# A Strassen feed-forward layer behind retention: the order in which the weights of the first layer are converted

## The chip, the cores and the metric

The kernel runs on one core of a Trainium2 chip. The metric is the device time of one execution in microseconds (us), from the first to the last work of the core. A core has five engines with a queue each, and every queue is worked off in the order in which the program issued it: TensorE (PE in the profile; its weight loads are shown apart as PEld), VectorE (DVE), ScalarE (ACT), GpSimd (POOL) and SyncE (SP), which here issues nearly all transfers. Engines wait for each other through semaphores.

## What is computed

Two layers, one behind the other (8 batches, 8 heads, 576 positions, head size 64; 4608 tokens, model width 512, inner width 2048):

```
scores = q k^T / sqrt(64);  ret = scores * gamma_h^(i-j) for i >= j, else 0;  attn = ret v
x = attn as [4608, 512]
h = max(x w_in, 0);  out = (h * h) w_out          # w_in 512 x 2048, w_out 2048 x 512
```

The two weights arrive as 64-bit floating point numbers. [...]the kernel converts them itself, with integer and 32-bit operations on the two halves of each number.

## The kernel before

**Stages.** Retention works through 40 chunks (per batch four of 128 positions and one of 64). Four chunks make a block of 512 tokens; there are nine blocks. The first layer of the feed-forward part runs beside retention. For block 0 it is a plain product (`first_in`, 16 of them, one per converted piece of 512 x 128 weights). Blocks 1 to 8 use Strassen's seven products (`ffn_in`, L758), whose inputs are sums of weight pieces and so need all of the weights. The second layer (`inner`, L1094) follows when retention is over.

**The order is written out by hand.** The program is under a manual schedule: each engine does its work in program order. The list of feed-forward products is `steps`; `step()` issues the next one. `convert(n)` issues the next n parts of the weight conversion. A prologue of single lines (L898 to L953) does chunks 0 to 3 and the first four pieces; then a loop over the chunks calls `ffn(i, half)` at the two halves of each chunk, which for block 0 issues one or two `first_in` and six conversion parts with each.

**One piece of the conversion** (`round_parts`, L213 to L231) has these parts:

- `one` (L213, VectorE): takes the exponent out of the high word.
- `two` (L217, VectorE): takes the upper fraction bits out of the high word.
- `beside` (L221 and L222, ScalarE, two instructions): makes a float of the low word, and a scale of the exponent. L222 needs `one` of the same piece; L221 needs only the loaded raw data.
- `three` (L225, VectorE): adds the two fractions; needs `two` and L221.
- `four` (L228, VectorE): multiplies by the scale; needs L222.
- `five` (L231, VectorE), issued by `last`: puts the sign on. After it the piece is ready for `first_in`, and `last` also asks for the next raw piece by a transfer.

In the kernel before, pieces 0 to 2 go one, two, beside, three, four, last. From piece 3 on `one` and `two` of the next piece are put between `beside` and `three` of this one (`N_ALONE`).

**What stands around it in the queues.** `first_in(j)` (L722) issues eight TensorE instructions of 128x512 (pieces 0 and 1 in halves and quarters), then the eviction of the result on ScalarE (`Relu`, L727), and puts the squaring (L730, VectorE) into a list from which the next product takes two. `turn` transposes a chunk's q and k on TensorE (L439) and copies them out of PSUM in two halves, with `(0, 1)` one on ScalarE and one on VectorE, with `(0, 0)` both on ScalarE (L450; L453 for chunks of 64). `scores_full` and `scores` (L547, L480) need both copies. `masked` (L492) or the mask in `scores_full` (L551) is VectorE's; `retain_full` (L573, L576) and the retain functions of the loop need it. `x_out` copies the chunk's result on ScalarE (L594), and `grown` the state (L506). `scale_q` (L385) and `scale_v` (L499) multiply loaded chunks by decays on GpSimd. `warm(n)` (L885) issues n products of 256 columns, of two TensorE instructions each, whose results nobody reads.

In the loop the parts of one call of `convert(6)` are three, four, last of a piece, beside of the next, and one, two of the one after that. In the first half of a chunk the six parts come ahead of the product, in the second half behind it.

Of the kernel before, what the change touches and what calls it, by code (L numbers as in the profile page):

```python
# [40 lines left out]
def kernel(  # L41
# [89 lines left out]
    N_EARLY = TOK // C  # L131

    def load(i, names="qkv"):
        b, ci, c0, cs = chunks[i]
        if i == 0:
            nc.sync.dma_start(dv, decays)
        got = loaded.setdefault(i, [None] * 3)
        for name, pool, src in (("q", ld3, q), ("k", ld5, k), ("v", ld4, v)):
            if name not in names:
                continue  # L140
            t = got["qkv".index(name)] = pool.tile([128, H, D], F32, tag=name, name=f"{name}_ld")

            issue = nc.scalar if i == 0 and name != "q" else nc.sync
            at = src[b, :, c0:c0 + cs, :].rearrange("h s d -> s h d")
            if name == "v":
                issue.dma_start(t[:cs], at)
            else:

                for e in range(2):
                    issue.dma_start(t[:cs, e * HP:(e + 1) * HP, :], at[:, e::2, :])  # L150
# [5 lines left out]
    pieces = [(0, m, e) for m in range(N_M) for e in range(2)]  # L156
    pieces += [(1, mq + mh * N_MQ, e) for mq in range(N_MQ) for mh in range(2) for e in range(2)]
    N_W1 = N_DF
    N_ALONE = 3
    N_HALF = 2  # L160
    stage = [W[5].rearrange("p (o s f) -> p o s f", o=4, s=NP),
             W[6][:, 0:3 * NP * 128].rearrange("p (o s f) -> p o s f", o=3, s=NP)]
# [5 lines left out]
    def raw_of(j):  # L168
        return raw_all[j % N_RAW] if j < N_W1 else raw_all[(j - N_W1) % 3]

    def exp_of(j):
        return exp_all[j % 2] if j < N_W1 else exp_all[2 * (j % 2)]
# [18 lines left out]
    def as_dst(j, t):  # L191

        if pieces[j][0] == 0:
            return t.rearrange("p (c f) -> p c f", c=N_DM)
        return t.rearrange("p (o s f) -> p o s f", o=2, s=2)
# [8 lines left out]
    def round_parts(j):  # L204
        words = raw_of(j).bitcast(U32).rearrange("p (n two) -> p n two", two=2)
        lo, hi = words[:, :, 0], words[:, :, 1]
        frac = raw_of(j).rearrange("p (n two) -> p n two", two=2)[:, :, 0]
        exp = exp_of(j).bitcast(U32)
        t = piece_dst(j)
        bits = t.bitcast(U32)  # L210

        def one():
            nc.vector.tensor_scalar(exp, hi, 20, 0x7FF, op0=ALU.logical_shift_right, op1=ALU.bitwise_and)  # L213

        def two():

            nc.vector.tensor_scalar(bits, as_dst(j, hi), 0xFFFFF, 0x100000, op0=ALU.bitwise_and, op1=ALU.bitwise_or)  # L217

        def beside():

            nc.scalar.activation(frac, lo, AF.Copy, scale=2.0 ** -52)  # L221
            nc.scalar.activation(exp, exp, AF.Relu, bias=exp_bias[:, 0:1], scale=2.0 ** 23)  # L222

        def three():
            nc.vector.scalar_tensor_tensor(t, bits, 2.0 ** -20, as_dst(j, frac), op0=ALU.mult, op1=ALU.add)  # L225

        def four():
            nc.vector.tensor_tensor(t, t, as_dst(j, exp_of(j)), op=ALU.mult)  # L228

        def five():  # L230
            nc.vector.scalar_tensor_tensor(bits, as_dst(j, hi), 0x80000000, bits, op0=ALU.bitwise_and, op1=ALU.bitwise_or)  # L231

        if not wide:
            to = t if pieces[j][0] == 0 else t.rearrange("p o s f -> p (o s) f")
            return [lambda: nc.sync.dma_start(to, piece_src(j))] + [lambda: None] * 5
        return [one, two, beside, three, four, five]
# [60 lines left out]

    def w_in_parts():

        parts = [round_parts(j) for j in range(N_W1)] + [[None] * 2]  # L300
        for j in range(N_W1):
            one, two, beside, three, four, five = parts[j]
            if j <= N_ALONE:
                yield from (one, two)
            yield beside
            if j >= N_ALONE:
                yield from parts[j + 1][0:2]
            yield three
            yield four

            def last(five=five):
                five()
                n_made[0] += 1
                if n_next[0]:
                    fetch_raw(2)

            yield last
# [3 lines left out]
    def convert(count):  # L321
        for _ in range(count):
            f = next(w_in_steps, None)
            f and f()
# [130 lines left out]
    def turn(i, engines=(0, 1)):  # L455
        turn_in(i)
        turn_out(i, engines)
# [99 lines left out]
    def carry_full(i):  # L557

        xp[0] = ps_x.tile([128, 2, 256], F32, tag="x", name="x_ps", padded_shape=[128, 2, 512])
        clean.clear()  # L560
        if chunks[i][1] == 0:
            u_ps[0] = ps_u.tile([128, HP, D], F32, tag="u", name="u_ps")
            return
        u = u_sb[2 * chunks[i][1] % 3]
        for hp, e, b in HEADS[0:2] + HEADS[4:6] + HEADS[2:4] + HEADS[6:8]:
            nc.tensor.matmul(x_full(hp, e, b), lhsT=u[rows(e), hp, :], rhs=st[i]["qT"][rows(e), hp, :],
                             start=clears(b, e), stop=False, skip_group_check=True)

    def retain_full(i):

        ci = chunks[i][1]
        for hp, e, b in (HEADS[j] for j in (0, 4, 2, 6, 1, 5, 3, 7)):
            nc.tensor.matmul(x_full(hp, e, b), lhsT=st[i]["vs"][:, head(hp, e), :], rhs=st[i]["ret"][:, e, hp, :],  # L573
                             start=clears(b, e), stop=False, skip_group_check=True)
        for hp, e, b in HEADS:
            nc.tensor.matmul(u_ps[0][rows(e), hp, :], lhsT=loaded[i][1][:, 2 * hp + e, :], rhs=st[i]["vs"][:, head(hp, e), :],  # L576
                             start=(ci == 0 and hp == 0), stop=(hp == HP - 1), skip_group_check=True)
        x_out(i, lambda: grown(i, 1))
# [232 lines left out]
    steps = []  # L811
# [12 lines left out]
    def step():  # L824
        n, f, *args = steps.pop(0)
        done[0] += 1
        f(*args)
# [14 lines left out]
    def ffn(i, half):  # L842

        gone[0] += chunks[max(0, min(i, N_CH - 1))][3] / 2
        if half == 2:
            gone[0] += chunks[min(i + 1, N_CH - 1)][3] / 2
        if steps and steps[0][0] == 0:

            move(6)
            for f in (step, lambda: convert(6)) if half else (lambda: convert(6), step):  # L850
                f()
            if half and i > N_EARLY and steps and steps[0][0] == 0:
                step()
                convert(6)
            return
        if not behind:
            behind.append((gone[0] - HALF, done[0]))
        points = behind + [p for p in PACE if p[0] > behind[0][0]]
        want = points[-1][1]
        for (x0, y0), (x1, y1) in zip(points, points[1:]):  # L860
            if gone[0] < x1:
                want = y0 + (y1 - y0) * (gone[0] - x0) / (x1 - x0)
                break
        count = max(1, int(want) - done[0])
        while steps and count:
            held[0] = half != 1 and count <= (1 if half else 2)

            if half == 2:
                due = sum(m[0] <= i + 2 for m in moves)
                move(max(2, min(4, -(-due // (count - 1)))) if count > 1 else 0)  # L870
            else:
                move(4 if half and len(moves) > 8 else 3 if half else 2 if count > 1 else 0)
            busy[0] = len(flips) > 0
            for f in flips[:1]:
                f()
            del flips[:1]
            step()
            count -= 1
        held[0] = busy[0] = False


    def warm(count):
        t = ps_f.tile([128, 512], F32, tag="f", name="idle_ps")
        for _ in range(count):
            nc.tensor.matmul(t[:, 0:256], lhsT=idle, rhs=idle[:, 0:1].to_broadcast([128, 256]), start=True, stop=True)  # L885
# [13 lines left out]
    scale_q(0, nc.vector)  # L899
    turn_in(0, (1,))  # L900
    scale_q(1, nc.gpsimd)
    warm(3)
    turn_in(0, (0,))
    turn_out(0)
    load(3)
# [2 lines left out]
    scores_full(0)  # L908
    turn(1, (0, 0))
    carry_full(0)  # L910
    retain_full(0)
    convert(3)
    scores_full(1)
    scale_q(2, nc.gpsimd)
    carry_full(1)
    convert(3)
    retain_full(1)
    load(4)
    fetch_raw(3)
# [6 lines left out]
    scale_q(3, nc.gpsimd)  # L926
    carry_full(2)
    first_in(1, (0,))
    convert(3)
    retain_full(2)  # L930
    load(6)
    turn(3)
    scores_full(3)
    scale_q(4, nc.gpsimd)
    convert(3)
    carry_full(3)
    for j in range(N_HALF):
        first_in(j, (1,), (0, C))
    early.close()
    ps_t[0] = first.enter_context(tc.tile_pool(name="ps_t", bufs=1, space=PS))  # L940
    retain_full(3)
    load(7)
    convert(5)
    step()
    step()
    turn(4)
    convert(3)
    step()
    scores(4)
    scale_q(5, nc.gpsimd)  # L950
    convert(6)
    step()
    convert(3)  # L953
    for i in range(N_EARLY + 1, N_CH + 1):
# [219 lines left out]
    for k in range(N_K + 1):  # L1174
# [5 lines left out]
        for e in range(3):  # L1180
# [8 lines left out]
            if sums_g:  # L1189
                f = sums_g.pop(0)  # L1190
            else:
                f = next(steps_0, None)
# [52 lines left out]
```

## Time and profile before

| what | value |
|---|---|
| median of three runs | 964.96 us (964.32 to 965.64) |
| span of the profiled execution | 963.2 us |
| PE, PEld busy | 98%, 88% |
| DVE, ACT, POOL busy | 81%, 35%, 14% |
| first product of block 0 to start (L722) | 18.0 us |
| last product of block 0 to start (piece 15) | 100.5 us |
| first product of block 1 to start (L758) | 105.7 us |

The table's last three rows come from the order of time: the conversion of the first weights and everything that the change touches lie in the first 106 us of 963 us. The rest of the span is block 1 to 8 of the first layer and the second layer, which the change leaves as they are. Where TensorE stands idle in those 106 us can be read from two views: the list of waits, limited to that stretch, and the order of time of one engine, which gives behind each group the idle time ahead of it and what ended it.

### The profile page before, as it was taken

To read this page: it belongs to the slowest core of one execution; us is meant where nothing else is said; L and a number is where in the kernel's file an instruction comes from. 1 tells how busy PE (TensorE), PEld (TensorE's weight loads), DVE (VectorE), ACT (ScalarE), POOL (GpSimd) and SP (SyncE) were. 2 spreads that over 40 slices of the span, in tenths; PEclk is the share of its full clock that TensorE was granted. 3 is DMA by queue.
4 is the path that set the end of the run, shared out by engine and by line. 5 is a ranking of instruction groups with operands and counts; after the bars stand their busy time and mean duration, and the time that the engine had idled before them with its cause. 6 is when DMAs were issued, how large, how long until landed. Compare 5 with 4: busy or idle time off the path is not lost. (4 is left out here: it accounts for less than half of the span.)

```text
span 963.2 us, 23158 instructions
## 1 busy us (share of the span) xinstructions
PE 947.4 (98%) x9754; PEld 849.4 (88%) x9754; DVE 784.6 (81%) x1446; ACT 337.4 (35%) x807; POOL 134.5 (14%) x123
## 2 busy tenths in 40 slices
PE   8999999999999999999999999999999999999998
PEld 6644688888888888888888899999999999999998
DVE  5788799888799887987966588888888787787876
ACT  3444375866765766667621010000000000000000
POOL 3311323214123123122110000000000000000000
PEclk9999999999999999999999999999999999999999
DMA  9983567676757867774278966445454454525251
GB/s 224 259 246 102 147 180 197 190 236 199 206 149 222 243 147 208 211 224 148 81 261 331 357 246 246 149 149 186 137 181 166 173 189 162 197 100 176 88 176 44
DMA packets 170728, 181.37 MB, mean 188 GB/s; under 512 B 116864, under 2 KB 131200, under 8 KB 163968
## 3 DMA queue, kind: packets, MB, share of 16 engines
q1 hardware_dynamic: 168528, 179.37, 59.5%
q8 instruction: 76, 1.25, 0.5%
q10 hardware_dynamic: 2096, 0.52, 0.3%
q14 instruction: 28, 0.23, 0.1%
HBM read 109.36 MB, written 70.52 MB: 187 GB/s over the span
## 5 line engine op out<-in xcount | busy, mean ns | idle before, releaser
L758 PE MATMUL h_b<-room,w 128*128 128x256 f32 x768 | 183.7, 382 | 2.3 <-DVE room L777 1.8
L422 ACT COPY qk<-flip 32x256 f32<-32x256 f32 x416 | 167.4, 402 | 6.1
L758 PEld LDWEIGHTS h_b<-room,w 128*128 128x128 f32 x768 | 144.1, 190 | 24.0 <-DVE room L777 3.3
L1094 PE MATMUL o_b<-w,room 128*128 128x128 f32 x1168 | 144.4, 275 | 0.2 <-DVE room L1046 0.2
L1094 PEld LDWEIGHTS o_b<-w,room 128*128 128x128 f32 x1168 | 137.3, 192 | 0.4 <-DVE room L1046 0.4
L1094 PE MATMUL o_c<-w,room 128*128 128x128 f32 x1008 | 123.0, 275 | 0.0
L758 PE MATMUL h_a<-room,w 128*128 128x256 f32 x512 | 122.1, 381 | 0.0
L758 PE MATMUL h_c<-room,w 128*128 128x256 f32 x512 | 121.7, 380 | 0.0
L1094 PEld LDWEIGHTS o_c<-w,room 128*128 128x128 f32 x1008 | 117.7, 192 | 0.0
L1108 ACT COPY r<-o_a 128x128 f32<-128x128 f32 x53 | 14.1, 266 | 271.6 <-PE o_a L1094 236.0
L758 PEld LDWEIGHTS h_a<-room,w 128*128 128x128 f32 x512 | 96.4, 190 | 13.8 <-issue 0.4
L758 PEld LDWEIGHTS h_c<-room,w 128*128 128x128 f32 x512 | 96.7, 190 | 13.3
L1094 PE MATMUL o_a<-w,a 128*128 128x128 f32 x688 | 85.6, 275 | 0.0
L775 POOL TENSOR_TENSOR room<-room 128x512 f32<-128x512 f32 x32 | 35.9, 1123 | 334.5 <-ACT room L774 334.5
L1094 PEld LDWEIGHTS o_a<-w,a 128*128 128x128 f32 x688 | 81.2, 192 | 0.1
L765 DVE SCALAR_TENSOR_TENSOR room<-room 128x512 f32<-128x512 f32 x96 | 70.6, 736 | 3.3
L722 PE MATMUL h_ps<-room,w 128*128 128x512 f32 (+2 forms) x160 | 59.9, 519 | 5.8 <-DVE w L231 5.6
L385 POOL TENSOR_TENSOR q_ld<-q_ld,dv 128x512 f32<-128x512 f32 (+1 forms) x39 | 46.4, 1189 | 85.7 <-DMA q_ld<-in_q_dram 85.5
L499 POOL TENSOR_TENSOR v_ld<-v_ld,dv 128x512 f32<-128x512 f32 (+1 forms) x40 | 52.9, 1323 | 6.7 <-DMA v_ld<-in_v_dram 6.7
L722 PEld LDWEIGHTS h_ps<-room,w 128*128 128x128 f32 x160 | 26.7, 190 | 30.2 <-issue 20.4
L617 PEld LDWEIGHTS x_ps<-qk,v_ld 64*64 64x64 f32 x1024 | 38.8, 134 | 13.0 <-issue 12.3
L777 DVE TENSOR_TENSOR room<-h_b,room 128x512 f32<-128x512 f32 x32 | 21.9, 685 | 33.5 <-PE h_b L758 33.5
(115 smaller groups left out, 1378.0 us busy)
## 6 DMA issues: line engine op xcount, KB each, us to landing
g_dram<-room SPq DMA_DIRECT2D x32, 1280.0 KB, 5.7
a<-g_dram SPq DMA_DIRECT2D x30, 1024.0 KB, 5.9
room<-g_dram SPq DMA_DIRECT2D x15, 1024.0 KB, 6.0
w<-w_dram SPq DMA_DIRECT2D x7, 1792.0 KB, 10.9
out_dram<-room SPq DMA_DIRECT2D x17, 512.0 KB, 3.2
q_ld<-in_q_dram SPq DMA_DIRECT2D x64, 128.0 KB, 5.3
w<-in_moe_w_in_dram SPq DMA_DIRECT2D x16, 512.0 KB, 6.4
w<-in_moe_w_out_dram SPq DMA_DIRECT2D x16, 512.0 KB, 4.1
```

The source lines that it names most:

```text
L385: engine.tensor_tensor(t, t, dv[:cs, :, NCH + ci:NCH + ci + 1].to_broadcast([cs, H, D]), op=ALU.mult)
L422: nc.scalar.copy(*moves.pop(0)[2:])
L499: nc.gpsimd.tensor_tensor(vs[:cs], vs[:cs], dv[:cs, :, ci:ci + 1].to_broadcast([cs, H, D]), op=ALU.mult)
L617: return [lambda hp=hp, e=e, b=b: nc.tensor.matmul(x_at(hp, e, b, h), lhsT=s["vs"][rows(h), head(hp, e), :], rhs=s["ret"][rows(h), e, hp, ...
L722: nc.tensor.matmul(p, lhsT=w[:, c, :], rhs=xT[0][:, c, :].rearrange("p (h t) -> p h t", h=2)[:, lo:hi, at[0]:at[1]], start=(c == 0), stop= ...
L758: nc.tensor.matmul(p[:, mm, :], lhsT=w[:, c, :], rhs=xs[n][right][:, c, :], start=(j in OPENS and mm == 0 and c == 0), stop=(j in CLOSES a ...
L765: nc.vector.scalar_tensor_tensor(t, t, 0.0, t, op0=ALU.max, op1=ALU.mult)
L775: nc.gpsimd.tensor_tensor(g["A11"], g["A11"], g["A11"], op=ALU.mult)
L777: nc.vector.tensor_tensor(g["A22"], p, p15, op=ALU.add)
L1094: nc.tensor.matmul(p, lhsT=s["lefts"][left][:, m, :], rhs=w_out[j][:, m, WO_SLOT[right], :], start=(i in OPENS and m == 0), stop=(i in CLO ...
L1108: nc.scalar.copy(r[:, 0, 0:128], p)
```

## The change

The order of the conversion's parts is changed, and nothing of what they compute.

- `w_in_parts` yields one, two, beside, three, four, last for every piece; `N_ALONE` goes.
- The prologue's calls of `convert` are cut and placed anew. Piece 0's first three parts stand ahead of the eviction of chunk 0 (in `retain_full(0)`) instead of behind it, its `three` follows there, and `four` and `last` come ahead of `retain_full(1)`. Piece 2 is converted ahead of `turn(3)` (before: its last three parts behind `scores_full(3)`), piece 3 ahead of `turn(4)` (before: its last three parts behind it), piece 4 and the first half of piece 5 ahead of the loop.
- In the loop a call of `convert(6)` is now three, four, last of a piece, then one, two, beside of the next: ScalarE's two instructions are issued at the call's end, a call ahead of the `three` that needs them. Every call stands ahead of its product, and so ahead of that product's eviction on ScalarE, in both halves of a chunk.
- The second `warm` call issues one product instead of three.

Its purpose is that weights are ready earlier, that ScalarE's parts don't wait behind evictions, and that fewer products are made for nothing.

```diff
-            one, two, beside, three, four, five = parts[j]
-            if j <= N_ALONE:
-                yield from (one, two)
-            yield beside
-            if j >= N_ALONE:
-                yield from parts[j + 1][0:2]
-            yield three
-            yield four
+            one, two, beside, three, four, five = round_parts(j)
+            yield from (one, two, beside, three, four)
...
             move(6)
-            for f in (step, lambda: convert(6)) if half else (lambda: convert(6), step):
-                f()
-            if half and i > N_EARLY and steps and steps[0][0] == 0:
-                step()
-                convert(6)
+            for _ in range(2 if half and i > N_EARLY else 1):
+                if steps and steps[0][0] == 0:
+                    convert(6)
+                    step()
...
-    warm(3)
+    warm(1)
...
     carry_full(0)
+    convert(3)
     retain_full(0)
-    convert(3)
+    convert(1)
     scores_full(1)
     scale_q(2, nc.gpsimd)
     carry_full(1)
-    convert(3)
+    convert(2)
     retain_full(1)
...
     first_in(1, (0,))
-    convert(3)
+    convert(2)
     retain_full(2)
     load(6)
+    convert(4)
     turn(3)
     scores_full(3)
     scale_q(4, nc.gpsimd)
-    convert(3)
     carry_full(3)
...
+    convert(2)
     retain_full(3)
     load(7)
-    convert(5)
+    convert(1)
     step()
     step()
+    convert(3)
     turn(4)
+    step()
     convert(3)
-    step()
     scores(4)
     scale_q(5, nc.gpsimd)
-    convert(6)
+    convert(3)
     step()
     convert(3)
```

More of the change, by code (lines that the diff above doesn't have):

```diff
@@ L158 @@
     N_W1 = N_DF
-    N_ALONE = 3
     N_HALF = 2
@@ L298, in w_in_parts @@
     def w_in_parts():
-        parts = [round_parts(j) for j in range(N_W1)] + [[None] * 2]
         for j in range(N_W1):
-            one, two, beside, three, four, five = parts[j]
-            if j <= N_ALONE:
-                yield from (one, two)
-            yield beside
-            if j >= N_ALONE:
-                yield from parts[j + 1][0:2]
-            yield three
-            yield four
+            one, two, beside, three, four, five = round_parts(j)
+            yield from (one, two, beside, three, four)
             def last(five=five):
```

## The prediction

> **What bounds the kernel now.** The page's first block gives PE 947.4 of 963.2 us. [...]in the slices, PEld stands at 4 to 8 tenths in the first four and at 8 or 9 later.
>
> ```profile
> PE 947.4 (98%) x9754; PEld 849.4 (88%) x9754; DVE 784.6 (81%) x1446; ACT 337.4 (35%) x807; POOL 134.5 (14%) x123
> ...
> PE   8999999999999999999999999999999999999998
> PEld 6644688888888888888888899999999999999998
> ```
>
> So I went to the waits. From 106 us on PE waits 2.5 us in all, and its chain runs to the end: time saved ahead of 106 us should shift everything behind it. Limited to the first 106 us the list of waits has:
>
> ```profile
> PEld h_ps L722 <- DVE w L231: 7.0, 5, 2.2
> PE h_ps L722 <- DVE w L231: 5.6, 6, 1.4
> ```
>
> L231 is the last part of a weight piece, L722 the product that reads it. PE itself loses 5.6 us in six waits; the 7.0 on PEld counts the same gaps from the last load. PE's order of time says which six:
>
> ```profile
> 18.04 1.97 PE L722 MATMUL h_ps<-room,w 128*128 128x256 f32 x8 [1.32 <-DVE w L231]
> ...
> 41.17 3.70 PE L722 MATMUL h_ps<-room,w 128*128 128x512 f32 x8 [0.26 <-DVE w L231]
> ...
> 46.18 3.70 PE L722 MATMUL h_ps<-room,w 128*128 128x512 f32 x8 [0.66 <-DVE w L231]
> ...
> 66.06 3.70 PE L722 MATMUL h_ps<-room,w 128*128 128x512 f32 x8 [1.38 <-DVE w L231]
> ...
> 80.79 3.70 PE L722 MATMUL h_ps<-room,w 128*128 128x512 f32 x8 [0.94 <-DVE w L231]
> ...
> 95.61 3.70 PE L722 MATMUL h_ps<-room,w 128*128 128x512 f32 x8 [1.04 <-DVE w L231]
> ```
>
> They are pieces 0, 3, 4, 8, 11 and 14. The last three are the second product of a second half, whose weights are finished between the two products: 1.38 + 0.94 + 1.04 = 3.36 us. VectorE is the reason, and it has a gap of its own each time:
>
> ```profile
> 57.42 0.69 DVE L450 COPY qk<-t_ps 128x512 f32<-128x512 f32 x1 [2.16 <-ACT qk L450]
> ...
> 61.96 1.13 DVE L730 TENSOR_TENSOR room<-room 128x512 f32<-128x512 f32 x1
> 63.02 1.54 DVE L225 SCALAR_TENSOR_TENSOR w<-w,w 128x512 f32<-128x512 uint32 x1
> ```
>
> The reader is to see the 2.16 us in which VectorE waits for ScalarE's half of the copies, and that the square (L730) runs ahead of the parts of piece 8.
>
> [...]the 2.16 us above stand with convertible data behind them. [...]L228 takes 0.69 us alone and 1.43 us at 38.22 beside GpSimd's L499. [...]the trace shows a granted clock of 1.00 throughout[...].
>
> **Prices.** By starts in VectorE's order of time: L213 and L217 0.33 and 0.34 us, L225 0.72, L228 0.73, L231 0.61, in all 2.73 us a piece; square, mask and copy 0.6 each. ScalarE: L221 0.57, L222 0.61, L727 0.50, L506 0.26, L450 0.6.
>
> **1, warm.** Before, six instructions fill 6.30 to 8.05 us, 0.29 each. The four removed are 1.17 us; q is scaled at 6.03 + 0.69 = 6.72, so the transposes start at 6.9 instead of 8.05. GpSimd's q of chunk 1 arrives by transfer at 8.20 and is ready at 9.26, its v at 10.28: chunk 0 comes some 1.1 us sooner, and not more.
>
> **2, pieces 0 and 1.** `one` of piece 0 can start at about 11.3 instead of 11.86 (raw data issued at 4.69, median landing 6.6 us). ScalarE's two parts now stand ahead of the chunk's copy, which then starts at 12.5 (before 12.71): the advance shrinks to 0.65 us at `retain_full(1)`. But `three` is done ahead of the mask, so behind the mask only L228 and L231 are left: ready near 16.35 instead of 17.9. The first product starts 1.65 us sooner (taking 1.32 away from its wait). Piece 1 is ready at 20, ahead of its product at 21.8.
>
> **3, the chain at chunk 3.** Here I expect the advance to be lost. Let T be the end of `first_in(1)`: before 25.4, now 23.75. Before, VectorE's copy waits only for the transposes and starts at 27.69; scores start at 28.5, T + 3.1. Now ScalarE does L727, then the chunk's copies once PE has finished (T + 1.15 and T + 1.65), then L221 from T + 1.95 and L222 from T + 2.5 to 3.2. VectorE has L225 from T + 2.65, L228 from T + 3.37, L231 from T + 4.1, and only then the copy, T + 4.7 to 5.4. Scores start at T + 5.5 = 29.25, 0.75 later than before.
>
> **4, to the loop.** Piece 3 is ready by 39 and its wait of 0.26 goes; with what else was tight there (0.36 at 33.97 for a copy that still comes at its time) I take 0.5 back: `first_in(3)` at 41.7 (before 41.17). Piece 4 has its parts behind the mask, 42.4 to some 45.8, since GpSimd's two multiplications at 42.7 to 45.6 are set by a transfer and still collide. PE arrives at 46.05. `first_in(4)` starts at 46.1 (before 46.18): the sum of steps 1 to 4 is 0.1 us, with 0.8 lost or 1.0 gained as ends.
>
> **5, the loop.** For pieces 5 to 7 the waits on VectorE are as before, and ScalarE's L222 now waits for `one` of the piece. Queued behind it are the previous L727, L506 and L450; L727 can be late by 2 us, since there are three PSUM buffers, one per product of 4.9 us; L450 is what VectorE's copy waits for. On entry both orders put this copy at 57.4. Then piece 8's parts no longer stand behind the square of product 7 (1.06 us by starts): ready at 65.0 instead of 66.0, and the wait of 1.38 falls to 0.35. In the next chunk the copy is ready 1 us sooner, the square is out of the way again, and piece 11 comes at 79.1 instead of 80.79. In the third, with no GpSimd work in the way, piece 14 starts at 92.8 instead of 95.61, without a wait. The advances are 1.05, 1.7 and 2.8 us. VectorE's load a chunk is 3 x 2.73 + 3 x 0.6 + 0.6 + 0.6 = 11.2 us, with about 1.5 for GpSimd 12.7, under PE's 13.6 (14.94 between products 6 and 9, less the 1.38): it can keep the advance, narrowly.
>
> **6, other edits.** The work of `fetch_raw` moves with `last`; pieces 14 and 15 are asked for at 54.65 and 60.63 and used past 85, so it is hidden by thirty us. Dropping `N_ALONE` moves L213 and L217 only. Behind 106 us nothing changes but the start; no transfer ends a PE wait there.
>
> Sum: 0.1 + 2.7 = 2.8 us, 964.96 - 2.8 = **962.2 us**.
>
> **Rivals.**
> B, more is kept: step 3 costs less because ScalarE's L221 runs earlier than I have it, all three loop waits go (3.36), and 0.6 of step 2 survives: 3.96, 961.0. For it: TensorE's six waits sum to 5.6. Against: step 3 rests on plain queue order.
> C, VectorE stays the bound: it is busy 9.79 of 10 us in the stretches 60 to 70 and 90 to 100, so parts moved ahead of a product push its squares and masks back, and the mask's readers wait instead. Only the square of one chunk is gained, 1.06, less 0.4 for step 3: 964.3.
> D, slower: step 3's 0.75 stays, and L222 ahead of L450 delays each of the turns of chunks 5 to 8 by its 0.6, so that VectorE's late copies pass it on to the weights: 0.75 + 2.4, less 1.06, is 2.1 more: 967.1. For it: the 2.16 us gap already ends at ScalarE's copy. Against: before, two such pairs stand between eviction and copy or next to it, and one of them now goes ahead of the eviction, when ScalarE idles 2.8 to 3.3 us for PE.
>
> **How the numbers follow.** My forecast has 0.55, B 0.17, C 0.18, D 0.10. Faster by over 0.2% is under 963.03: B, and 0.48 of the forecast (its entry bound of 0.8 lost leaves 963.0), 0.65; within 0.2% is C and the other 0.07 of the forecast, 0.25; slower is D, 0.10. The range 960.7 to 964.5 runs from just past B to just past C and leaves out D and the tails.
>
> **What would show it.** Product 0 of L722 at about 16.4 us; VectorE's copy for chunk 3 behind L231 and scores at 29 us or later; products 8, 11 and 14 at 65, 79 and 93 us with waits on L231 near 0.4, 0.3 and none; product 15 at 97.7; DVE's wait for L450 under 1.5 us in chunks 7 and 8. It is wrong if step 3's scores start by 27.5, if L551 or L492 or L450 end new PE waits in the loop, or if an advance at 106 us isn't found in the span's end.

## The result, and the profile after

The changed kernel takes 969.43 us (median; 967.91 to 969.82) where the kernel before takes 965.29 beside it: a ratio of 1.0042 [1.0024, 1.0059], slower by 4 us. The forecast was 962.2 with a range from 960.7 to 964.5. In the profiled executions the spans are 967.7 and 963.2 us. Lines below the first edits have moved: the product is now L714 (L722 before), its eviction L719 (L727), the square L722 (L730), the parts L212, L216, L220, L221, L224, L227, L230, the copy of transposes L442 (L450), block 1's product L750 (L758).

The page's first block of the kernel after shows PE's busy time up by 2.2 us, with four matmuls fewer. The same work takes longer somewhere.

```profile
PE 949.6 (98%) x9750; PEld 851.4 (88%) x9750; DVE 786.7 (81%) x1446; ACT 337.0 (35%) x807; POOL 134.9 (14%) x123
```

The lists of waits of the first 106 us, before and then after: the wait for finished weights on PE fell from 5.6 to 3.0 us, as intended. PE's wait for VectorE's copy of the transposes grew from 1.2 to 3.6 us, which takes nearly all of that back. ScalarE's wait for `one` of the same piece grew from 0.5 to 24.7 us.

```profile
PE sc_ps L547 <- DVE qk L450: 1.2, 2, 0.9
...
ACT w L222 <- DVE w L213: 0.5, 1, 0.5
```
```profile
ACT w L221 <- DVE w L212: 24.7, 11, 3.9
...
PE sc_ps L539 <- DVE qk L442: 3.6, 2, 3.4
...
PE h_ps L714 <- DVE w L230: 3.0, 4, 1.2
```

PE's order of time after. Of the six waits shown of before, those at pieces 0, 8 and 14 are left, shorter; those at pieces 3, 4 and 11 are gone, and piece 15 has a new one. The wait at chunk 3 is the longest:

```profile
17.24 1.97 PE L714 MATMUL h_ps<-room,w 128*128 128x256 f32 x8 [1.17 <-DVE w L230]
...
30.18 1.16 PE L539 MATMUL sc_ps<-qk 64*128 64x128 f32 x16 [3.35 <-DVE qk L442]
...
32.33 3.14 PE L714 MATMUL h_ps<-room,w 128*128 128x128 f32 x16
...
37.18 2.05 PE L714 MATMUL h_ps<-room,w 128*128 128x128 f32 x16 [0.22 <-ACT room L586]
...
67.37 3.70 PE L714 MATMUL h_ps<-room,w 128*128 128x512 f32 x8 [0.55 <-DVE w L230]
...
95.70 3.70 PE L714 MATMUL h_ps<-room,w 128*128 128x512 f32 x8 [0.81 <-DVE w L230]
101.11 3.70 PE L714 MATMUL h_ps<-room,w 128*128 128x512 f32 x8 [0.44 <-DVE w L230]
```

Set against the starts of before, this gives the offsets (after less before):

| work | before | after | offset |
|---|---|---|---|
| product of piece 0 | 18.04 | 17.24 | -0.8 |
| scores of chunk 3 | 28.52 | 30.18 | +1.7 |
| `retain_full(3)` | 32.20 | 35.40 | +3.2 |
| product of piece 4 | 46.18 | 48.31 | +2.1 |
| product of piece 8 | 66.06 | 67.37 | +1.3 |
| product of piece 15 | 100.51 | 101.11 | +0.6 |
| block 1's first product | 105.68 | 106.29 | +0.6 |
| at 400 us | | | +0.2 |
| behind the pause at 416 us | | | +2.8 |
| behind 424 us, and at the end | | | +4.5 |

So the loop of the first layer wins back nearly all that chunk 3 loses, and then 4.3 us go at a place which the change doesn't touch. Time per stretch shows what the two places have in common. In the windows of the kernel after (stretch, busy us and instructions of PE, PEld, DVE, ACT and POOL, granted clock, DMA share, GB/s), PEclk stands at 0.83 in the stretch at or behind each pause; before, it is 1.00 in all four.

```profile
20.00:30.00 10.00, 5.81 (x88) 4.83 (x88) 5.97 (x11) 3.84 (x8) 2.96 (x3) 1.00 1.11 225
30.00:40.00 10.00, 9.60 (x105) 8.74 (x106) 4.10 (x10) 3.11 (x9) 3.50 (x4) 0.83 0.98 241
410.00:420.00 10.00, 7.31 (x153) 6.48 (x152) 9.03 (x15) 4.81 (x11) 3.44 (x3) 1.00 1.02 278
420.00:430.00 10.00, 10.00 (x40) 8.49 (x40) 3.39 (x7) 6.21 (x14) 1.32 (x2) 0.83 0.37 134
```

The clock record of the trace has the stretches exactly: half clock from 31.22 to 34.63 us and from 420.34 to 423.75, 3413 ns each. In the second one a 128x256 matmul of L750 starts every 427 ns, just ahead of it and behind it every 216: its 3.4 us hold what takes 1.7 at full clock. Two lines of PE's order of time above show it on products of one kind: sixteen 128x128 matmuls take 3.14 us at 32.33 and 2.05 at 37.18.

**Chunk 3.** ScalarE and then VectorE in the order of time of the kernel after. ScalarE puts both parts of piece 2 ahead of its half of the copies. VectorE waits for the first of them, and its own half of the copies stands behind all three of its parts:

```profile
26.51 0.67 ACT L220 ACTIVATE w<-w 128x512 f32<-128x512 uint32 x1
27.07 0.72 ACT L221 ACTIVATE w<-w,exp_bias 128x512 uint32<-128x512 uint32 x1
27.68 0.58 ACT L442 COPY qk<-t_ps 128x512 f32<-128x512 f32 x1
```
```profile
27.21 0.69 DVE L224 SCALAR_TENSOR_TENSOR w<-w,w 128x512 f32<-128x512 uint32 x1 [2.41 <-ACT w L220]
28.01 0.69 DVE L227 TENSOR_TENSOR w<-w,w 128x512 f32<-128x512 f32 x1
28.74 0.69 DVE L230 SCALAR_TENSOR_TENSOR w<-w,w 128x512 uint32<-128x512 uint32 x1
29.35 0.68 DVE L442 COPY qk<-t_ps 128x512 f32<-128x512 f32 x1
```

The weights of piece 2, for which this is done, are needed only after 39 us: the products at 32.33 and 37.18 are those of pieces 0 and 1.

**416 us.** What PE shows after the pause, in its order of time, and its wait in the list behind 106 us:

```profile
419.17 1.02 PE L750 MATMUL h_a<-room,w 128*128 128x256 f32 x4 [2.69 <-issue]
```
```profile
PE h_a L750 <- issue: 2.7, 1, 2.7
```

"issue" means that PE waited for nothing that the profile shows: no semaphore, no data. What falls into this pause is in the transfers. One queue, q8, carries 76 packets of the kind "instruction" with 1.25 MB, so 16 KB each. In the kernel before, the 38th of them starts at 412.0 us, when PE has begun 9654 records. In the kernel after it starts at 416.64, when PE has begun 9921 and already stands still, and takes 1.03 us; PE's next matmul starts 1.5 us behind its end. For PE's 19,500 records (9750 matmuls and 9750 loads) 76 packets are one for every 257, so I take each to be a block of PE's instructions; no view names the engine that they are for. The DMA views of the kernel before in the stretch 411 to 413 us, and of the kernel after in 416 to 418 (packets, MB, share of 16 engines), each have the block:

```profile
q8 instruction: 1, 0.02, 3.0%
```
```profile
q8 instruction: 1, 0.02, 3.2%
```

The kernel after has none on q8 in 411 to 413 us. SyncE issues loads of q and k there, but their data don't move yet. Ahead of them stands a write of 1344 KB, converted weights of the second layer (`w_dram`, L283), issued at 410.08. The views of the kernel after for 405 to 411 us and for 411 to 413:

```profile
w_dram<-w SPq DMA_DIRECT2D x1, 1344.0 KB, 6.8
```
```profile
DMA packets 273, 0.76 MB, mean 381 GB/s; under 512 B 16, under 2 KB 16, under 8 KB 272
```

In the trace the write is 384 packets of 3584 bytes, and the loads are packets of 256 bytes; between 411 and 413 us only 16 packets are under 512 bytes. The write's packets run from 411.56 to 416.46 us, the loads' start at 416.0, and the block starts at 416.64, when the write is over. In the kernel before, the same write runs from 411.38 to 416.70, and the block starts 0.6 us after its first packet.

### The profile page after: what moved, and what is told of

Same layout as the page of the kernel before. It is cut to its first block, busy times and chain, and to the rows that moved or that the text cites. A ratio compares the mean times of both kernels' runs of the same rounds, so it can differ in the third digit from the quotient of the medians.

```text
span 967.7 us, 23162 instructions
## 1 busy us (share of the span) xinstructions
PE 949.6 (98%) x9750; PEld 851.4 (88%) x9750; DVE 786.7 (81%) x1446; ACT 337.0 (35%) x807; POOL 134.9 (14%) x123
## 3 DMA queue, kind: packets, MB, share of 16 engines
q8 instruction: 76, 1.25, 0.5%
## 5 line engine op out<-in xcount | busy, mean ns | idle before, releaser
L750 PE MATMUL h_b<-room,w 128*128 128x256 f32 x768 | 184.7, 384 | 2.1 <-DVE room L769 1.8
L750 PEld LDWEIGHTS h_b<-room,w 128*128 128x128 f32 x768 | 145.1, 191 | 24.5 <-DVE room L769 3.2
L750 PE MATMUL h_a<-room,w 128*128 128x256 f32 x512 | 122.6, 382 | 2.7 <-issue 2.7
L750 PE MATMUL h_c<-room,w 128*128 128x256 f32 x512 | 121.7, 380 | 0.0
L750 PEld LDWEIGHTS h_a<-room,w 128*128 128x128 f32 x512 | 96.6, 190 | 16.0 <-issue 2.6
L750 PEld LDWEIGHTS h_c<-room,w 128*128 128x128 f32 x512 | 96.7, 190 | 13.3
L714 PE MATMUL h_ps<-room,w 128*128 128x512 f32 (+2 forms) x160 | 60.7, 528 | 3.3 <-DVE w L230 3.0
L714 PEld LDWEIGHTS h_ps<-room,w 128*128 128x128 f32 x160 | 27.9, 199 | 27.5 <-issue 20.6
```

Of the source, the lines that this page charges most:

```text
L714: nc.tensor.matmul(p, lhsT=w[:, c, :], rhs=xT[0][:, c, :].rearrange("p (h t) -> p h t", h=2)[:, lo:hi, at[0]:at[1]], start=(c == 0), stop= ...
L750: nc.tensor.matmul(p[:, mm, :], lhsT=w[:, c, :], rhs=xs[n][right][:, c, :], start=(j in OPENS and mm == 0 and c == 0), stop=(j in CLOSES a ...
```

## The experiments

Two theories stood at the start. **The first**: two losses, independent of each other. The order at chunk 3 makes a pause which also lowers the clock, and the four TensorE instructions (two unread products) that were removed make a block of instructions late. **The rival**: the new order costs ScalarE and VectorE time all along, and the place at 416 us only shows it. In the expectations, theory 1 is the pause at chunk 3, theory 2 the late block of instructions. Each run was timed beside the kernel before, which had medians of 964.92 to 965.03 us.

**Chunk 3 alone.** From the kernel after, piece 2 goes behind the scores:

```diff
-    convert(4)
     turn(3)
     scores_full(3)
     scale_q(4, nc.gpsimd)
+    convert(4)
     carry_full(3)
```

> The kernel after, with the four parts of piece 2 moved from ahead of turn(3) to behind scores_full(3) and scale_q(4). Theory 1 (the chain at chunk 3 costs the prologue its advance and, by the 3.35 us pause, one slow-clock stretch of 3.4 us): scores of chunk 3 start near 27.5 us, no slow-clock stretch near 31 us, and the first product of block 1 starts at about 102.5 to 103.5 us instead of 106.3. If the pause near 416 us is independent of that (theory 2, a late block of TensorE's instructions), it may stay, and the time is 966 to 967; if it goes, 961 to 963. Rival (the loop's order is at fault, ScalarE waiting for L212): the first product of block 1 stays at 105.5 us or later.

Measured: 965.49 us, 1.0006 [0.9998, 1.0014]. PE's order of time for it:

```profile
27.15 1.16 PE L539 MATMUL sc_ps<-qk 64*128 64x128 f32 x16 [0.91 <-DVE qk L442]
...
28.84 2.05 PE L714 MATMUL h_ps<-room,w 128*128 128x128 f32 x16
```

The pause is 0.91 instead of 3.35, the product that took 3.14 us takes 2.05, and block 1 starts at 102.01, which is 4.28 earlier than in the kernel after. Of these, 0.58 were there before chunk 3 (the first product starts at 16.66 instead of 17.24, with the same instructions up to there), so chunk 3's order is worth some 3.7 us. The pause of 2.7 us near 412 us stays, and has a cause of its own. (The profile is that of the fastest run; eleven of the thirteen have a mean clock of 0.998, one slow stretch, where the profiled run has none.)

**The unread products back.** From the kernel after:

```diff
-    warm(1)
+    warm(3)
```

> The kernel after, with three products in the second warm call as before, so that TensorE's program has the instruction count of the kernel before. Theory 2 (the pause near 416 us comes from where the blocks of TensorE's instructions begin, which two products fewer have moved by four): the pause of 2.7 us near 416 us goes, and the span is about 963.5 to 965 us, with the prologue's loss still there. Rival (the pause comes from the times at which transfers collide, not from the count): pause stays or comes and goes, 968 to 970. The advance from warm, 0.7 us at the first product, goes in both.

Measured: 966.50, 1.0013 [1.0006, 1.0020]. The 38th block starts at 412.4 with 9654 records begun, there is no pause there, and the offset at block 1 (+0.4) is nearly the offset at the end (+0.6). The pause at chunk 3 and its slow clock stay. So each loss stays when the other is taken away.

**The unread products alone.** The same edit by itself, in the kernel before:

```diff
-    warm(3)
+    warm(1)
```

> The kernel before, with one product instead of three in the second warm call, nothing else. Theory 2: TensorE's program is four instructions shorter and the pause near 416 us appears, 967 to 969. Rival: no pause, 964 to 965; the 0.7 us of advance at the first product is used up by the waits for weights and brings 0 to 0.7 us.

Measured: 968.69, 1.0040 [1.0027, 1.0054]: taking two products away makes the kernel 3.7 us slower. Block 1 starts 0.3 earlier, at 400 us the kernel is 0.7 ahead, then PE stands still for 2.7 us at 415.6 and the block starts at 415.9 (9921 records). Four of the five runs have a mean clock of 0.998, and they are the slower four.

**One product instead of two removed.** In the kernel before, `warm(2)`:

> The kernel before with two products instead of three in the second warm call: four instructions fewer on TensorE, half of what e3 took away. [...]If that is enough to fall behind the loads that start at 410.4 us: pause of 2 to 3 us, 967 to 969. If there is room: no pause, 964.5 to 965.3.

Measured: 964.16, 0.9992 [0.9985, 0.9999]. The block starts at 411.5 with 9650 records begun, no pause. It is a step: four TensorE records fewer cost nothing, eight cost a pause.

**The load out of the block's way.** From the kernel with `warm(1)`, the loads of q and k of chunk 37 and v of chunk 36 are issued some products later:

```diff
-            loads(i)
+            if i != 33:
+                loads(i)
...
             ffn(i - 1, 2)
+            if i == 33:
+                loads(i)
```

> The kernel of e3 (before, second warm call cut to one product), with one group of loads moved: q and k of chunk 37 and v of chunk 36, which start at 410 to 416 us, are issued behind that chunk's feed-forward products instead of ahead of them. TensorE's program is that of e3. If the pause is a block of TensorE's instructions queued behind these loads: the block comes at 412 to 414 us, the pause of 2.6 us is under 1 us or gone, 964.2 to 966. If the block is simply asked for late, whatever the transfers do: the pause stays at 2.6 us, 967 to 969.

Measured: 965.42, 1.0005 [0.9997, 1.0014], 3.3 us less than with the load in its old place. The block starts at 414.5 instead of 415.9. PE's wait in the list, 400 to 425 us, first with the load in its old place, then with it later:

```profile
PE h_a L758 <- issue: 2.7, 1, 2.7
```
```profile
PE h_a L758 <- issue: 1.3, 1, 1.3
```

I expected under 1 us and got 1.3; the rest of the gain goes with the clock: ten of the twelve runs have a mean clock of 1.0, where four of the five with `warm(1)` alone have 0.998. Data traffic is thus part of the cause of the late block. The traces point at one transfer: the write of 1344 KB is still there, and the block starts as its last packet ends.

| kernel | the write's packets, us | block starts |
|---|---|---|
| before | 411.38 to 416.70 | 412.01 |
| after | 411.56 to 416.46 | 416.64 |
| `warm(1)` alone | 410.68 to 415.47 | 415.88 |
| `warm(1)`, loads later | 410.55 to 414.49 | 414.49 |

With the loads away the write takes 3.9 us instead of 4.8 and ends 1.0 us earlier, which is most of the 1.4 us by which the block is earlier. The same holds in every profile here: in the nine kernels without the pause the block starts 0.5 to 0.7 us after the write's first packet, in the five with it 0.0 to 0.4 us after its last. No run moved the write itself, so this is read from traces and not tested by an edit.

**The pause filled.** From the kernel after, unread products between `turn(3)` and `scores_full(3)`; this leaves the order of the queues as it is and keeps PE busy:

```diff
     turn(3)
+    warm(4)
     scores_full(3)
```

> The kernel after with four more unread products of 256 columns between turn(3) and scores_full(3), where TensorE stands idle for 3.35 us. Nothing else; the chain of copies there stays. If the pause lowers TensorE's clock: no slow-clock stretch near 31 us, the products there take 2.05 instead of 3.14 us for 16, and the first product of block 1 starts 0.5 to 1.5 us sooner than 106.3. TensorE's program is eight instructions longer than that of before, so the pause near 416 us should go by theory 2: 963.5 to 965. If the clock was not set by the pause: slow stretch stays, and 965 or more.

Measured: 963.97, 0.9991 [0.9981, 1.0002]; that is 5.5 us under the kernel after. PE's order of time:

```profile
25.86 2.00 PE L876 MATMUL idle_ps<-w 128*128 128x256 f32 x8
...
29.27 1.16 PE L539 MATMUL sc_ps<-qk 64*128 64x128 f32 x16 [1.41 <-DVE qk L442]
```

The scores still wait for the same copy, but no slow stretch follows: the sixteen matmuls of 128x128 behind it take 2.05 us. Nine of its twelve runs have a mean clock of 0.999 or 1.0; none of the four of the kernel after has. Block 1 starts at 104.92, 1.4 earlier than in the kernel after and 2.9 later than with piece 2 behind the scores. The order in the queues thus costs some 3 us by itself. The clock's share is what remains, and the run doesn't give its size, since its start was 0.9 earlier as well (first product at 16.35). With these eight matmuls the pause near 416 us is gone as well; most of the 5.5 us is that.

**Piece 2 ahead of `turn(3)` in the kernel before.** The same place as in the change, with `one`, `two` and `beside` already done:

```diff
     load(6)
+    convert(3)
     turn(3)
     scores_full(3)
     scale_q(4, nc.gpsimd)
-    convert(3)
     carry_full(3)
```

> The kernel before, with three, four and last of piece 2 ahead of turn(3) instead of behind scores_full(3), nothing else. ScalarE's two parts of piece 2 stay ahead of chunk 2's evictions. By the chain: VectorE's copy for chunk 3 behind L231 at 28.5 to 28.7 us, scores at 29.3 instead of 28.5, a pause of about 1.8 us[...]; VectorE has less to do later, so that 0 to 0.5 us come back: first product of block 1 at 106.0 to 106.5, 965.3 to 966. If the loss at chunk 3 in after came from ScalarE alone: scores at 28.5, no change.

Measured: 966.86, 1.0021 [1.0013, 1.0029]. Its order of time on PE and its window:

```profile
29.52 1.84 PE L547 MATMUL sc_ps<-qk 64*128 64x128 f32 x16 [1.85 <-DVE qk L450]
```
```profile
30.00:40.00 10.00, 9.78 (x104) 8.40 (x101) 5.37 (x11) 3.45 (x9) 3.42 (x3) 0.84 0.97 227
```

I had counted no slow clock behind this pause. In the profile it follows, the sixteen matmuls of the scores taking 1.84 us instead of 1.16, and 14 of the 20 runs have a mean clock of 0.998 or less; the other six are the six fastest, at 965.5 to 966.3.

**The loop's calls alone.** In the kernel before, every call of `convert(6)` goes ahead of its product, and nothing else changes:

```diff
-            for f in (step, lambda: convert(6)) if half else (lambda: convert(6), step):
-                f()
-            if half and i > N_EARLY and steps and steps[0][0] == 0:
-                step()
-                convert(6)
+            for _ in range(2 if half and i > N_EARLY else 1):
+                if steps and steps[0][0] == 0:
+                    convert(6)
+                    step()
```

> The kernel before, with only the loop's calls changed: each call of six parts ahead of its product in both halves of a chunk. Prologue, warm and the order of the parts as before. If the loop's part of the prediction holds (the waits of products 8, 11 and 14 shrink), the first product of block 1 starts 2 to 3 us sooner than 105.7, and the time is 962 to 963; count of instructions as before, so no pause near 416 us by theory 2. Rival (VectorE is the bound in the loop, and the order there brings nothing): 105 to 106 us, 964 to 965.

Measured: 960.95, 0.9959 [0.9947, 0.9972]. Pieces 8 and 14 are there without a wait, 11 waits 0.47; block 1 starts 4.1 us sooner, and the whole 4.1 arrives at the end.

**The parts' order on top of it.** To the previous kernel, the order of the parts in the change (one, two, beside, three, four, last, for each piece):

```diff
-            one, two, beside, three, four, five = parts[j]
...
+            one, two, beside, three, four, five = round_parts(j)
+            yield from (one, two, beside, three, four)
...
-    convert(5)
+    convert(3)
```

> The kernel of e4 (before, with the loop's calls ahead of the products), with the parts in the order of the kernel after: one, two, beside, three, four, last for each piece, so that in the loop each call ends with one, two, beside of the next piece. Count of instructions as before. If ScalarE's waiting for L212 (24.7 us in after, in front of evictions and copies) costs TensorE time: first product of block 1 at 102.3 to 103.5 us instead of 101.6, and 961.5 to 963. If it is hidden: 960.6 to 961.4.

Measured: 964.45, 0.9993 [0.9982, 1.0003]; block 1 starts at 104.80, so 3.2 of the 4.1 us are gone, more than expected. ScalarE's order of time in it:

```profile
55.79 0.72 ACT L221 ACTIVATE w<-w,exp_bias 128x512 uint32<-128x512 uint32 x1 [1.95 <-DVE w L212]
56.42 0.57 ACT L719 ACTIVATE room<-h_ps 128x512 f32<-128x512 f32 x1
56.90 0.36 ACT L498 COPY u_sb<-u_ps 128x256 f32<-128x256 f32 x1
57.15 0.59 ACT L442 COPY qk<-t_ps 128x512 f32<-128x512 f32 x1
```

The scale (L221) stands still for VectorE's `one`, and the eviction, the state and the copy run behind it without a wait of their own. VectorE in turn waits for the copy, and its parts come later. VectorE's order of time, with the old order of parts and then with the new one:

```profile
56.05 0.69 DVE L450 COPY qk<-t_ps 128x512 f32<-128x512 f32 x1 [0.57 <-ACT qk L450]
```
```profile
57.78 0.69 DVE L442 COPY qk<-t_ps 128x512 f32<-128x512 f32 x1 [1.08 <-ACT qk L442]
```

From 44 to 104 us these waits sum to 0.8 us in two with the old order and to 4.2 in four with the new one. What reaches PE is its wait for finished weights in the same stretch, which grows by 2.5 of the 3.2 us lost:

```profile
PE h_ps L722 <- DVE w L231: 0.5, 1, 0.5
```
```profile
PE h_ps L714 <- DVE w L230: 3.0, 4, 0.9
```

For the loop the rival theory is thus right in part: the new order of parts costs time there. The edit shows the cost; that it goes by way of L221 is read from the traces.

**The good parts together.** To the loop's calls alone, `warm(1)`, and the two unread products put back where PE waits at chunks 2 and 3, so that the number of instructions stays:

```diff
-    warm(3)
+    warm(1)
...
     turn(2, (0, 0))
+    warm(1)
     scores_full(2)
...
     turn(3)
+    warm(1)
     scores_full(3)
```

> The kernel before with the loop's calls ahead of the products (as in e4) and the second warm call cut to one product, but with the two products put back later: one behind turn(2), one behind turn(3), where TensorE waits 1.3 and 1.0 us for copies. TensorE's instruction count is that of the kernel before. If the pause near 416 us follows the count of instructions and not the warm call as such: no pause, and 960.2 to 961.0. If it follows from starting 0.7 us earlier: the pause is there, 963 to 965.

Measured: 960.23, 0.9950 [0.9935, 0.9966]. Block 1 starts at 100.34, the block of instructions at 406.4 with 9654 records begun, no pause.

**The same without the two put back:**

> The kernel of e5 without the two products that were put back: second warm call of one product, the loop's calls ahead of the products. TensorE's program is eight instructions shorter. By the count theory the block of instructions comes late near 411 us, with a pause of 2 to 3 us: 962 to 964, against 960.2 for e5, though the prologue has less to do. If the pause belongs to the times of e3 and after alone: 959.8 to 960.6.

Measured: 964.02, 0.9987 [0.9980, 0.9994], with a pause of 2.7 us at 412.4 (9921 records): 3.8 us over the previous kernel, from two unread products fewer.

**Piece 0 further forward as well**, added to the kernel with the good parts together:

```diff
-    retain_full(0)
     convert(3)
+    retain_full(0)
+    convert(1)
...
-    convert(3)
+    convert(2)
     retain_full(1)
```

> The kernel of e5 (before, the loop's calls ahead of the products, two unread products moved behind turn(2) and turn(3)), with piece 0's parts forward as in the kernel after: three ahead of retain_full(0), one behind it, two ahead of retain_full(1). Count of instructions as before. Piece 0 should be ready 0.7 to 1.2 us sooner (first product near 16.3 us instead of 17.1), and the gain lasts to the loop, where piece 0 no longer matters: 959.4 to 960.2. Rival (another wait takes it up, as the 1.07 us at piece 10): 960 to 960.7, like e5.

Measured: 959.69, 0.9939 [0.9924, 0.9954]. The first product starts at 16.4, 0.7 earlier, but block 1 at 100.26 against 100.34: the loop had eaten the advance, and the two versions can't be told apart by their times. Both beat the kernel before and the kernel after.

## Why the prediction was wrong

From -2.8 us to +4.5 us, by its own steps, with the offsets above:

| step | forecast's error, us |
|---|---|
| 1 and 2, the start | +0.9 |
| 3, slow clock left out | +1.5 |
| 4, to the loop | -0.2 |
| 5, the loop | +1.2 |
| 6, "Behind 106 us nothing changes but the start" | +4.3, and -0.4 from 106 to 400 us |

The sum is 7.3, as it should be.

**Steps 1 and 2** were right in kind, and their size was the execution's. In the profile of the kernel after, transposes start at 7.42, not at 6.9, and the first product at 17.24, not at 16.35. But two other kernels have the same instructions up to there, and their first products start at 16.66 (piece 2 behind) and at 16.35 (pause filled), the predicted time. In these two the pair of unread matmuls ahead of the transposes of q takes 0.70 us (at 5.47 and 5.98). In the kernel after it takes 1.19, at 6.30, and the clock record has full clock only from 7.33. The 0.9 is spread at the start, which the prediction had no term for. A reading ahead of the steps is slightly off: PEld stands at 4 to 6 tenths in the first four slices and at 6 in the fifth, at 8 or 9 only behind it. Nothing rests on that.

**Step 3** had the mechanism and its arithmetic right. The copy was to start at T + 4.7, where T is the end of `first_in(1)`; T was 24.7 and the copy started at 29.35, T + 4.65. The scores' start at 30.18 instead of 29.25 is the error of T, the start's 0.9. What failed is that the sum has no slow clock. The granted clock of 1.00 throughout was true of the trace of before, where PE's longest pause in the first 106 us is 1.38; but step 3 itself made a longer one, 3.35 as it came, and didn't ask what would follow. The clock's cost should have stood in the sum as an unknown with two ends, 0 and 1.7 us.

**Step 4** regained 1.1 us where it counted on 0.85. Its own terms don't agree by 0.3: 0.75 lost and 0.5 taken back put `first_in(3)` at 41.4, where it has 41.7.

**Step 5** gained 1.5 us of the 2.7 forecast. The calls ahead of products were under-priced: they alone give 4.1 us. The order of the parts was priced at nothing: the step names the queue behind L222, the scale, but takes the copy to come at 57.4 in both orders and the eviction to have 2 us to spare. With the calls moved, the copy came at 56.05 with the old order of parts and at 57.78 with the new one; the scale stood waiting, with eviction and copy behind it, and took back 3.2 us. This is the mechanism of rival D, with the sign of D on one part of the change. The sign that the forecast named for this step came true all the same: none of VectorE's waits for this copy is over 1.2 us, where under 1.5 was named. That sign couldn't tell a good loop from a better one.

**Step 6** failed most. The removed products were priced as time on PE only. Without them PE has eight records fewer, and one block came late, at 416.64 us instead of 412.01: 2.7 us of pause, and 1.7 of slow clock behind it. What stands ahead of the prediction, that the change leaves the rest of the span as it is, fails at the same point. The kernel with `warm(1)` alone shows it, `warm(3)` in the kernel after takes it away. The sentence "no transfer ends a PE wait there" looked at transfers that PE's semaphores name; the profile names none for a block of instructions.

Rival D's 967.1 was nearest to the time, but by adding up other things. Its first term, 0.75 from step 3, was small beside what chunk 3 cost, and it had nothing at 416 us.

**Open.** What sets the start of a block was not shown, so it isn't shown either why it starts behind the write in five kernels and near the write's beginning in nine. A write under way doesn't always hold it up: in the kernel before, other blocks start 4.7 and 2.1 us into the writes of weights at 207 and 499 us, before these are over. Eight records fewer shift PE's work by some 0.86 us there (the time of records 9646 to 9654 in the kernel before); whether this shift is what makes the block late was not shown. And ten of the 21 runs of the kernel after with `warm(3)` have a mean clock of 0.996, by its size two slow stretches, where its profile shows one.

## What to carry to other kernels

Work that is moved forward must not pass the half of a copy for which the next matmuls wait: put it behind that copy (some 3.7 us here), and on the engine that feeds a second one, keep what waits for the other engine behind evictions and copies (3.2 us here). Where PE must wait, fill the wait with products that nobody reads, or count a slow stretch of the clock as possible: here one followed pauses of 1.85, 2.7 and 3.35 us in profiled executions, and none followed in the one where the 3.35 was filled down to 1.41. After a change in the number of PE instructions, look along the whole span for waits on "issue" and see whether an instruction block came late (2.7 us here), and which large transfer was under way; a shift of the same size everywhere is not to be taken for granted, and edits of this kind are best timed one by one, since here one part gave 4.1 us while three others took more than that away.

## What the runs showed of the hardware

**When a pause lowers the clock.** In the clock record of the kernel after, full clock lasts from 7.33 to 31.22 us, 23,893 ns or seven times the 3413 of a slow stretch, and the next full stretch 385,706 ns, 113 times. Counting PE's records in the 3413 ns ahead of each slow stretch, PE was idle for a share of 0.68 (chunk 3) and 0.66 (416 us) in the kernel after, 0.74 at chunk 3 with `warm(3)`, and 0.53 with piece 2 ahead in the kernel before (some hundredths depend on which records are counted). The length of the pause didn't decide alone: 2.7 us at a late block lowered the clock in the profile of the kernel after and left it at 1.0 in those of `warm(1)` alone, of the loop's calls with `warm(1)` and of piece 2 behind the scores, while 1.85 us lowered it with piece 2 ahead (0.84 from 30 to 40 us). So the same pause comes with a slow stretch, 1.7 us, in one execution and with none in the next, and the last four of these kernels have runs of 0.998 and of 1.0 side by side; what decides between the two was not shown.

**Instruction blocks.** PE stood still for 2.7 us in four of the kernels profiled here whose 38th block was late (after, `warm(1)` alone, `warm(1)` with the loop's calls, and piece 2 behind), each time with the block's packet starting at 9921 records begun, where it otherwise started at about 9654. In a fifth, with the loads later, it started at 9826 and PE stood still for 1.3 us. In all five the start followed the end of a write of 1344 KB by 0.0 to 0.4 us.
